# Recommender cross network on one core: first chunk in two halves with the weights loaded between them, clock products on a constant, two products moved into the last wait

## The chip, the cores and the metric

One core of a Trainium2 chip. The metric is the device time of one execution in microseconds (us); lower is better. Every execution is listed with its time and with the span from its first to its last instruction; the time is 1.75 to 1.98 us more than the span. All executions here are of the state "fast".

## The reference, cut to what matters

```python
B, F, D, L = 16384, 26, 16, 6        # Din = 416
x = x0
for l in range(L):
    proj = jnp.einsum('bd,de->be', x, ws[l]) + bs[l]
    x = x0 * proj + x
return x
```

All tensors are bf16. The kernel holds x with the 416 features on partitions, as three tiles of 128 (t = 0, 1, 2) and a tail of 32, and works on 8 groups of 2048 rows, each of four chunks of 512 rows.

## The kernel before

A small scheduler takes instructions with what they read and write and derives the waits; a PSUM bank is one unit of dependence. The front: load the first chunk in two halves, then the first layer's weights; keep TensorE busy with products of ones until data come, so that its clock rises; transpose the first chunk, copy it out of PSUM, and start the products of the first two output tiles.

```python
load_nat(0, 0, 2)                    # chunk 0, rows k = 0, 1 of each four: 208 KB
load_nat(0, 2, KK)                   # chunk 0, k = 2, 3: 208 KB
load_wm(0, "sp")                     # weights of layer 0: 312 KB
for j in range(1, NJ): ...           # chunks 1 to 3, in halves
...
def keep_busy(n, b):                 # clock products, up to four blocks of 128 columns at once
    ... h.matmul(bank(b, ...), ones[:, :], ones[:, :].unsqueeze(1).broadcast_to([P, m, P]), start=True, stop=True),
        reads=["ones"], writes=[("ps", b)]
keep_busy(22, 7)
def first_job():
    transposed_chunk(0)              # 6 transposes, keep_busy(2), 6 transposes, 3 copies of 512 columns
    ...                              # 7 small transposes of the bias, one copy
    keep_busy(5, 3)
    full(g, l, 0, ba, True, True, chunks=[0])      # 3 products of 512 columns
    full(g, l, 1, bb, True, True, chunks=[0])      # 3 more
    transposed_chunk(1)              # 12 transposes, 3 copies
    transposed_chunk(2)
    full(g, l, 0, ba, True, True, chunks=[1]) ...
```

The back, the last layer of the last group, with rows on partitions, so that the result can be stored without a transpose: four rounds kk of four sums; each sum is three products of 416 columns (one per t) and two thin ones. ScalarE copies each sum out (nat_out), VectorE multiplies by x0 and adds x (nat_mul, nat_add), and a store follows each round.

```python
turn_tails(b0); nat_rows(0, bks[0], False)
turn_last(0, b1); turned_out(0, b1)  # 8 transposes that wait for the last additions of the tile before; a copy on VectorE
for j in range(NJ):
    if j == 2: turn_last(2, b2)
    nat_full(0, j, bks[0][j], False, (2,)); nat_out(0, j, bks[0])
turned_out(2, b2)                    # a copy of 1024 columns on ScalarE
...
for kk in range(1, KK):
    nat_rows(kk, bks[kk])
    for j in range(NJ):
        nat_full(kk, j, bks[kk][j], False); nat_out(kk, j, bks[kk]); ...
```

## Time and profile before

| | before |
|---|---|
| median of the first 3 executions | 475.43 us (475.24 to 475.45) |
| median of 6, when the change was measured (those 3 and 3 more) | 475.44 us (475.13 to 476.41) |
| the execution that was profiled | 477.81 us, span 476.0 us |
| TensorE busy | 99% of the span |

### The profile page before, as it was taken

To read this page: it belongs to the slowest core of one execution; us is meant where nothing else is said; L and a number is where in the kernel's file an instruction comes from. 1 tells how busy PE (TensorE), PEld (TensorE's weight loads), DVE (VectorE), ACT (ScalarE), POOL (GpSimd) and SP (SyncE) were. 2 spreads that over 40 slices of the span, in tenths; PEclk is the share of its full clock that TensorE was granted. 3 is DMA by queue.
4 is the path that set the end of the run, shared out by engine and by line. 5 is a ranking of instruction groups with operands and counts; after the bars stand their busy time and mean duration, and the time that the engine had idled before them with its cause. 6 is when DMAs were issued, how large, how long until landed. Compare 5 with 4: busy or idle time off the path is not lost.

```text
span 476.0 us, 8464 instructions
## 1 busy us (share of the span) xinstructions
PE 470.3 (99%) x3407; PEld 200.9 (42%) x3407; DVE 404.2 (85%) x699; ACT 342.0 (72%) x372; POOL 6.3 (1%) x15
## 2 busy tenths in 40 slices
PE   8999999999999999999999999999999999999996
PEld 4434444654444444444444444444444444444442
DVE  1798888888888888898889869988888888888897
ACT  3677777777777777777777777777777777777776
POOL 1000000000000000000000000000000000001000
PEclk9999999999999999999999999999999999999999
DMA  8986830650001398469409940890001029125899
GB/s 223 171 173 143 185 88 1 110 113 1 19 16 30 65 240 147 67 134 239 111 12 170 240 102 10 175 289 2 1 1 35 0 56 232 34 45 101 222 175 288
DMA packets 138651, 53.18 MB, mean 112 GB/s; under 512 B 112362, under 2 KB 138100, under 8 KB 138612
## 3 DMA queue, kind: packets, MB, share of 16 engines
q1 hardware_dynamic: 138456, 52.54, 49.9%
q8 instruction: 26, 0.43, 0.4%
q14 instruction: 13, 0.11, 0.1%
q10 hardware_dynamic: 156, 0.11, 0.1%
HBM read 5.97 MB, written 13.63 MB: 41 GB/s over the span
## 4 chain that ended last, share of the span: by engine, by line
PE 96%; DMA 2%; ACT 1%; DVE 1%; SPq 0%; issue 0%; DVEq 0%
PE ps L471 78%; PE ps L492 7%; PE ps L513 7%; PE ps L868 1%; PE ps L486 1%; DMA wm<-in_ws_dram 1%; ACT tw L398 1%; PE ps L504 1%; PE ps L592 1%; DMA ot<-x 1%; DVE tw L407 0%; PE ps L879 0%; ACT x L923 0%; DVE x L929 0%; DVE x L935 0%; PE ps L912 0%
## 5 line engine op out<-in xcount | busy, mean ns | idle before, releaser
L398 ACT ACTIVATE tw<-ps,bias 128x1024 bf16<-128x1024 f32 (+1 forms) x295 | 299.8, 1071 | 119.5 <-PE ps L492 81.1
L471 PE MATMUL ps<-x,wm 128*128 128x512 bf16 (+1 forms) x1755 | 380.9, 373 | 0.5 <-DMA wm<-in_ws_dram 0.5
L471 PEld LDWEIGHTS ps<-x,wm 128*128 128x128 bf16 x1755 | 165.3, 98 | 210.0 <-issue 29.3
L407 DVE TENSOR_TENSOR tw<-tw,x 128x1024 bf16<-128x1024 bf16 (+1 forms) x285 | 192.7, 684 | 51.8 <-ACT tw L398 51.2
L412 DVE TENSOR_TENSOR x<-tw,x 128x1024 bf16<-128x1024 bf16 (+1 forms) x285 | 182.6, 681 | 0.0
L492 PE MATMUL ps<-x,w 32*128 32x512 bf16 x512 | 39.2, 379 | 0.0
L513 PE MATMUL ps<-x,wm 128*32 128x512 bf16 x564 | 33.0, 380 | 0.0
L438 ACT ACTIVATE ts<-ps,bias 128x512 bf16<-128x512 f32 x47 | 28.8, 701 | 0.0
L442 DVE TENSOR_TENSOR x<-ts,x 128x512 bf16<-128x512 bf16 x47 | 18.7, 419 | 3.9 <-DMA x<-x 3.8
L513 PEld LDWEIGHTS ps<-x,wm 128*32 128x32 bf16 x564 | 13.8, 96 | 17.6 <-issue 5.3
L492 PEld LDWEIGHTS ps<-x,w 32*128 32x128 bf16 x512 | 7.8, 92 | 26.9 <-issue 26.4
L440 DVE TENSOR_TENSOR ts<-ts,x 128x512 bf16<-128x512 bf16 x47 | 18.6, 419 | 0.0
L602 DVE COPY x<-ps 128x512 bf16<-128x512 bf16 x5 | 2.0, 423 | 10.7 <-PE ps L592 10.7
L712 POOL COPY ost<-ot 128x512 bf16<-128x512 bf16 x6 | 4.8, 805 | 424.3 <-DMA ot<-x 424.3
L868 PE MATMUL ps<-wm,x 128*128 128x416 bf16 x48 | 9.5, 340 | 0.0
L604 ACT ACTIVATE x<-ps 128x512 bf16<-128x512 bf16 x7 | 3.8, 595 | 7.4 <-PE ps L592 7.4
L923 ACT ACTIVATE x<-ps 128x416 bf16<-128x416 f32 x16 | 7.8, 526 | 1.6 <-PE ps L868 1.5
L868 PEld LDWEIGHTS ps<-wm,x 128*128 128x128 bf16 x48 | 4.3, 98 | 4.2 <-issue 1.0
L504 PE MATMUL ps<-x,w 32*32 32x512 bf16 x188 | 5.9, 374 | 0.0
L486 PE MATMUL ps<-x,w 32*32 32x512 bf16 x208 | 5.6, 385 | 0.0
L929 DVE TENSOR_TENSOR x<-x,x 128x832 bf16<-128x832 bf16 (+1 forms) x10 | 4.9, 502 | 0.6 <-ACT x L923 0.4
L935 DVE TENSOR_TENSOR x<-x,x 128x832 bf16<-128x832 bf16 (+1 forms) x9 | 4.7, 540 | 0.2
(41 smaller groups left out, 35.4 us busy)
## 6 DMA issues: line engine op xcount, KB each, us to landing
out_dram<-ost SPq DMA_DIRECT2D x6, 1664.0 KB, 7.0
x<-x SPq DMA_DIRECT2D x24, 96.0 KB, 2.1
wm<-in_ws_dram SPq DMA_DIRECT2D x6, 312.0 KB, 3.4
x<-in_x_dram SPq DMA_DIRECT2D x8, 208.0 KB, 4.8
x<-in_x_dram SPq DMA_DIRECT2D x4, 416.0 KB, 8.3
out_dram<-ost SPq DMA_DIRECT2D x2, 832.0 KB, 5.5
x<-x SPq DMA_DIRECT2D x22, 64.0 KB, 2.0
out_dram<-x SPq DMA_DIRECT2D x3, 416.0 KB, 4.1
```

The source lines that it names most:

```text
L398: add("act", lambda h, a=a, w=w, b0=b0: h.activation(tw[r][:, a * CH:(a + w) * CH], psum[:, b0 * CH:(b0 + w) * CH], ACT_F.Identity, bias=b ...
L407: add("dve", lambda h, a=a, e=e: h.tensor_tensor(tw[r][:, a * CH:e * CH], tw[r][:, a * CH:e * CH], x0s[s0][:, i * GC + a * CH:i * GC + e * ...
L412: add("dve", lambda h, a=a, e=e: h.tensor_tensor(xs[so][:, i * GC + a * CH:i * GC + e * CH], tw[r][:, a * CH:e * CH], src(i, a, e), ALU.ad ...
L438: add("act", lambda h: h.activation(ts[r][:, :], bank(b), ACT_F.Identity, bias=bias[:, 3, l:l + 1], scale=1.0), reads=[("ps", b), "bias"], ...
L440: add("dve", lambda h: h.tensor_tensor(ts[r][:, :], ts[r][:, :], x03, ALU.mult), reads=[("ts", r)] + tok0, writes=[("ts", r)], release=True)
L442: add("dve", lambda h: h.tensor_tensor(x3s[so][:, :], ts[r][:, :], res, ALU.add), reads=[("ts", r)] + rtok, writes=[("x3", so), ("x3", so, ...
L471: add("pe", lambda h, t=t, j=j, k=k, w=w: h.matmul(bank(banks[j])[:, k * w:(k + 1) * w], wm[l][:, t, ecols], src(t, j, j + 1)[:, k * w:(k ...
L486: add("pe", lambda h, q=q, j=j, r=r, c=c, o=o: h.matmul(psum[o, banks[j] * CH:(banks[j] + 1) * CH], w3[l][q, i * P + c * T32:i * P + (c + ...
L492: add("pe", lambda h, q=q, j=j, r=r: h.matmul(bank(banks[j]), w3[l][q, ecols], src[q, :], start=first and not inner, stop=not first and no ...
L504: add("pe", lambda h, l=l, b=b, s3=s3, ri=ri, qi=qi, ro=ro, qo=qo: h.matmul(psum[qo, b * CH:(b + 1) * CH], w3[l][qi, NT * P:D], s3[qi, :], ...
L513: add("pe", lambda h, t=t, j=j, src=src, l=l, b=b, ro=ro, qo=qo: h.matmul(psum[qo, b * CH:(b + 1) * CH], wm[l][:, t, NT * P:D], src(t, j, ...
L868: add("pe", lambda h, t=t: h.matmul(bank(b, n=D), xcol(t, j, kk), wm[l][:, t, :], start=(first and t == 0), stop=(not first and t == NT - 1)),
```

## The change

Its intent, as far as the diff shows it: let TensorE start real products before the second half of the first chunk is there, start the clock products without waiting for Pool's ones, and put two products of the second round into TensorE's wait for the last tile.

```diff
     load_nat(0, 0, 2)
+    load_wm(0, "sp")
     load_nat(0, 2, KK)
-    load_wm(0, "sp")
...
     def keep_busy(n, b):
+        one = nc.const_aps.tensor(1.0, [P, CH], BF16)
...
-                bank(b, n=m * P).rearrange("p (m c) -> p m c", m=m), ones[:, :],
-                ones[:, :].unsqueeze(1).broadcast_to([P, m, P]), start=True, stop=True),
-                reads=["ones"], writes=[("ps", b)])
+                bank(b, n=m * P), one[:, 0:P], one[:, 0:m * P], start=True, stop=True), writes=[("ps", b)])
-    keep_busy(22, 7)
+    keep_busy(25, 7)
...
-        transposed_chunk(0)
+        first_half(0)               # 6 transposes, 3 copies of 256 columns
...
-        keep_busy(5, 3)
+        keep_busy(4, 3)
-        full(g, l, 0, ba, True, True, chunks=[0])
-        full(g, l, 1, bb, True, True, chunks=[0])
+        half_products(0, ba[0], 0)  # 3 products of 256 columns
+        first_half(1)
+        half_products(1, bb[0], 0)
+        half_products(0, ba[0], 1)
+        half_products(1, bb[0], 1)
...
     nat_rows(0, bks[0], False)
+    nat_full(1, 1, bks[1][1], True, (0, 1))    # two products of round 1, taken out of it below
     turn_last(0, b1)
```

More of the change, by code (lines that the diff above doesn't have):

```diff
@@ L583, in transposed_chunk @@
     def transposed_chunk(j):
-        ba, bb = ((0, 1), (3, 0), (6, 7), (0, 1))[j]
+        ba, bb = ((3, 0), (6, 7), (0, 1))[j - 1]
         s = slot(0)
-        place = ((ba, 0), (bb, 0), (ba, CH)) if j == 0 else ((ba, 0), (ba, CH), (bb, 0))
+        place = ((ba, 0), (ba, CH), (bb, 0))
         for k2 in (0, 2):
@@ L594, in transposed_chunk @@
                         reads=[("nat", j, k), x0_tok(nat, 0, 0), "ident"], writes=[("ps", b)])
-            if j == 0 and k2 == 0:
-                keep_busy(2, 3)
         for t in range(NT):
@@ L604, in transposed_chunk, with half_cols, first_half, half_products @@
                 add("act", lambda h, dst=dst, sp_=sp_: h.activation(dst, sp_, ACT_F.Copy), **kw)
+    HC = CH // 2
+    def half_cols(t, h):
+        return slice(t * GC + h * HC, t * GC + (h + 1) * HC)
+    def first_half(h):
+        ba, bb = ((0, 1), (5, 6))[h]
+        s = slot(0)
+        place = ((ba, 0), (bb, 0), (ba, HC))
+        for t in range(NT):
+            b, o = place[t]
+            for k in (2 * h, 2 * h + 1):
+                c = slice(o + (k - 2 * h) * P, o + (k - 2 * h + 1) * P)
+                add("pe", lambda h_, t=t, k=k, b=b, c=c: h_.transpose(
+                    psum_t(b)[:, c], x0n[:, 0, k, t * P:(t + 1) * P], ident[:, :]),
+                    reads=[("nat", 0, k), x0_tok(nat, 0, 0), "ident"], writes=[("ps", b)])
+        for t in range(NT):
+            b, o = place[t]
+            dst, sp_ = x0s[s][:, half_cols(t, h)], psum_t(b)[:, o:o + HC]
+            kw = dict(reads=[("ps", b)], writes=[("x0h", t, h)] + ([x0_tok(s, t, 0)] if h else []))
+            if b == bb:
+                add("act", lambda h_, dst=dst, sp_=sp_: h_.activation(dst, sp_, ACT_F.Copy), **kw)
+            else:
+                add("dve", lambda h_, dst=dst, sp_=sp_: h_.tensor_copy(dst, sp_), **kw)
+    def half_products(i, b, h):
+        s = slot(0)
+        for t in range(NT):
+            add("pe", lambda h_, t=t: h_.matmul(
+                bank(b)[:, h * HC:(h + 1) * HC], wm[0][:, t, i * P:(i + 1) * P], x0s[s][:, half_cols(t, h)],
+                start=(t == 0 and h == 0), stop=False),
+                reads=[("x0h", t, h), ("wm", 0)], writes=[("ps", b)])
     def transposed_tails(b):
@@ L907, in turn_tails, with nat_rows @@
             j += n
-    def nat_rows(kk, bks, first=True):
+    def nat_rows(kk, bks, first=True, begun=()):
         for j in range(NJ):
@@ L912, in nat_rows @@
             add("pe", lambda h, j=j, q=q, r=r: h.matmul(
-                bank(bks[j], n=D), x3col(j, kk), w3[l][q, :], start=first, stop=False, tile_position=(r * T32, 0)),
+                bank(bks[j], n=D), x3col(j, kk), w3[l][q, :], start=first and j not in begun, stop=False, tile_position=(r * T32, 0)),
                 reads=tok3 + [("w3", l, r)], writes=[("ps", bks[j])])
@@ L970, in bass_standalone__cross_network_dcn__recsys_kernel @@
     for kk in range(1, KK):
-        nat_rows(kk, bks[kk])
+        begun = (1,) if kk == 1 else ()
+        nat_rows(kk, bks[kk], begun=begun)
         for j in range(NJ):
-            nat_full(kk, j, bks[kk][j], False)
+            nat_full(kk, j, bks[kk][j], False, (2,) if j in begun else range(NT))
             nat_out(kk, j, bks[kk])
```

## The prediction

> **What bounds the kernel now.** I read the page first, for the share of each engine and for the chain that ended last; then the chain and the timeline of the first 17 us and of the last 15 us, because the order of instructions shows the same ones in both kernels between the first chunk of group 0 and the closing stage.
>
> ```profile
> PE 470.3 (99%) x3407; PEld 200.9 (42%) x3407; DVE 404.2 (85%) x699; ACT 342.0 (72%) x372; POOL 6.3 (1%) x15
> PE 96%; DMA 2%; ACT 1%; DVE 1%; SPq 0%; issue 0%; DVEq 0%
> ```
>
> TensorE is the bound from about 6.5 us to about 470 us. The change takes no product out of that stretch: nearly the same products run, some cut in two. So only the two ends, some 6.5 us and 6 us, can move. This is the chain of waits at the front:
>
> ```profile
> 1.65 4.67 DMA wm<-in_ws_dram
> 6.46 2.72 PE ps L471 x6
> 9.18 1.97 PE ps L592 x24
> 11.16 1.29 PE ps L471 x6
> ```
>
> The first products wait for the weights: issued at 1.65 us, 4.67 us under way, landed at 6.32. Then six products of 512 columns take 2.72 us, while the next six of the same kind take 1.29 us. TensorE thus runs at half speed at first. The timeline shows the rest of it:
>
> ```profile
> 0.99 2.53 PE L572 MATMUL ps<-ones 128*128 128x512 bf16 x6 [0.99 <-POOL ones L522]
> 3.38 0.82 PE L592 MATMUL ps<-ident,x 128*128 128x128 bf16 x6
> 4.20 0.85 PE L592 MATMUL ps<-ident,x 128*128 128x128 bf16 x6
> 5.27 0.71 PE L572 MATMUL ps<-ones 128*128 128x512 bf16 x2
> 6.46 2.72 PE L471 MATMUL ps<-x,wm 128*128 128x512 bf16 x6 [0.48 <-DMA wm<-in_ws_dram]
> 8.97 2.18 PE L592 MATMUL ps<-ident,x 128*128 128x128 bf16 x24
> ```
>
> The clock products wait for Pool to write the ones (0.99). Both halves of the first chunk are turned and copied out before the weights come, so only the weights hold PE, with 0.48 us of full idleness. Among the 24 transposes at 8.97 the mean of one changes from 314 to 219 ns at 10.3 us: that is where the clock rises in this execution.
>
> At the back the chain is:
>
> ```profile
> 462.08 0.40 PE ps L879 x4
> 462.48 0.35 PE ps L868 x2
> 462.83 0.65 PE ps L879 x8
> 463.48 0.35 PE ps L868 x2
> 464.30 2.22 PE ps L868 x12
> 470.86 0.53 ACT x L923
> 471.41 0.39 DVE x L929
> 471.81 0.59 DVE x L935
> ```
>
> The transposes of the last tile wait for VectorE's additions (x L412); then three rounds of twelve products run, and at the very end ScalarE and VectorE finish the last quarter.
>
> **What the Trainium skill says.** "TensorE: Matmul & The Clock Gate", Part 1 (the HAM clock gate): the array starts at half rate, a free-running window of about 3.4 us decides, and the point of the rise differs from run to run. The trace agrees on the two rates: 512 columns follow each other at about 0.42 us early (six from 6.46 to 8.97, where the transposes start) and at 0.215 us later (1.29/6). The same page, Part 4 (PE-mode transpose), says that transposes do not count as busy; the trace speaks against that, since the 3.4 us before the rise were 2.0 us of products and 1.4 us of transposes, without a gap. "DMA: Bandwidth & Descriptors", section "Queues, rings and completion order": on each DMA engine descriptors are consumed in ring order. The trace agrees roughly: first half-chunk, second half-chunk, weights landed in the order of issue, at about 3.3, 3.8 and 6.3 us. "PSUM — Partial Sum Buffer", section "The four PSUM rules": the first product of a group clears the marks of its whole bank, which lets the second 256 columns start without the flag; no cost follows from it, and no run so far shows it.
>
> **The change part by part, the front.**
> 1. Weights second in the queue. The issue moves from 1.65 to 1.20 us, and 208 KB fewer lie ahead of it. In the trace the second half-chunk lands some 0.5 us after the first (3.83 against 3.33), so the weights should land about 0.5 us earlier: 6.32 - 0.5 = 5.8 us (estimate). The second half-chunk now follows them. The bytes ahead of the pair's end are unchanged, so it lands where the weights did, about 6.3 us. The loads after them do not move.
> 2. What PE has to do after that. Before: six products at half speed, 2.51 us from 6.46 to 8.97. I take half of one for 256 columns (0.21 us) and a quarter for a transpose of 128 (0.107, as the twelve that start from 8.97 to 10.15 are spaced). After: three products (0.64), six transposes (0.64), and nine more products (1.92): 3.2 us from about 5.97, so 9.17; or, if the second half's landing binds, 6.4 + 0.64 + 1.92 = 8.96. The transposes that were hidden ahead of the weights now lie behind them and eat the gain of 0.5 us: 0 to 0.2 us later.
> 3. Copies. Two VectorE copies of 256 columns and one on ScalarE per half. VectorE took 425 ns for 512 and 683 for 1024, so about 0.30 us for 256; ScalarE 597 and 1030, so 0.38 us (estimates from these rows). Since the dependence is on the whole bank, both VectorE copies wait for the last transpose. At half speed the first products of the second tile (0.64 us) cover this. At full speed they do not (0.33 us), and 0.1 us shows; I make it 0.25 us later then.
> 4. The constant. PE needs no ones from Pool, so it starts at about 0.74 us instead of 0.99; 25 blocks of 128 columns at 0.107 = 2.67 us, ending at 3.40 where before 22 ended at 3.34. Nothing on the path gets shorter by this. Its use is only that the clock may rise earlier. Against that, PE now stands idle from about 4.9 to 5.9 us (half the transposes and one clock product are gone from there), about twice the former gap.
>
> Front without a change in the clock: +0.1 to +0.25 us.
>
> **The back.** Two products of 416 columns (2.22 us for twelve in the chain, so about 0.18 each, 0.35 to 0.37 together) move ahead of the transposes. PE has idle pieces there of about 0.24, 0.09 and 0.11 us, read from the single instructions between 461.6 and 463.1, so they fit nearly whole. They need the last bank that ScalarE empties (about 461.7), hence start some 0.1 us late. The rounds of products then end about 0.32 us earlier. But the ends of the second round are taken by ScalarE, which is held by its copy of 1024 columns until 465.4 and does not move, and VectorE works almost without pause from 466.4. I followed its instructions to the last multiplication that waits for ScalarE, at 471.41: it can come at 471.2. So about 0.15 us of the 0.35 reaches the end.
>
> Sum with an equal clock: +0.15 - 0.15 = 0, in 475.4 us.
>
> **The rivals.** (a) The clock rises earlier. The 9.4 us that PE ran at half rate hold 3.9 us after the weights; full speed there saves at most 1.9 us. For it: if 10.38 us, where the records put the rise, is the end of a window of the skill's 3.41 us, the windows before it are 0.15 to 3.56 and 3.56 to 6.97; in the first PE was busy 2.57 us, 75%, and with the earlier start it is about 83% (0.25 us more of 3.41); if the threshold lies between, the rise comes at 3.56. The next loads allow it: the last half-chunk of the 24 transposes landed at 8.5 us, the next group's data 2 us before use. That gives about 473.5. (b) The clock rises later in more runs, because of the longer gap. The three runs agree within 0.21 us, which may mean that they, unlike the profiled one, rose before 6 us; then losing that costs up to 1.9 us: about 477. (c) The weights do not land earlier, because other transfers slow them: then PE pays the transposes in full, +0.64 us at half speed: 476.0. (d) The moved products in the back save all 0.35 us, if ScalarE's order lets VectorE follow: 475.2.
>
> **Range and chances.** Equal clocks give 475.1 to 475.7, which I hold at about 60%. The earlier start was surely made for the clock, so I give (a) more than (b), and put the point a little below no change, at 475.2 us. The range 473.6 to 476.6 takes in most of (a), all of (c) and half of (b). Two per cent are 9.5 us; both ends together hold not much more than that of waiting, so faster or slower by over 2% are at 0.01 each.
>
> **What would show it.** In the changed profile: clock products from 0.74 us; the weights' wait ended near 5.8 us; an idle piece of about 1 us ahead of the first 256-column products; their last one ended near 9.1 us (right), near 8 us (the clock rose before), or near 9.6 (c). The place at which 314 ns transposes or 634 ns products become 219 and 379 decides (a) and (b). In the back: two products before the transposes and the last ScalarE copy to last VectorE addition shifted by 0.15 us against the last tile's additions. I am wrong if the front gains over 0.3 us at an equal clock, or if the times lie under 474 without an earlier rise.

## The result, and the profile after

The changed kernel took 476.09 us (median of 6, 475.70 to 477.58), the kernel before 475.44 us. The ratio of the fast runs is 1.0014, with a 95% interval from 0.9999 to 1.0030: the same, leaning to slower. Ratios are the mean time of one kernel's fast runs over that of the other's of the same rounds, so not quite the ratio of the medians.

The timeline of TensorE at the front, kernel after (start, length, line, operation, count, and in brackets the length of the wait before it and what ended it; the bias's small transposes and one clock product at 3.86 to 4.5 us are left out):

```profile
0.77 2.82 PE L573 MATMUL ps<-const-bfloat16-1.0 128*128 128x512 bf16 x7 [0.77 <-PEq L1039]
3.39 0.54 PE L617 MATMUL ps<-ident,x 128*128 128x128 bf16 x6
4.45 0.49 PE L632 MATMUL ps<-x,wm 128*128 128x256 bf16 x3
6.11 0.51 PE L617 MATMUL ps<-ident,x 128*128 128x128 bf16 x6 [1.16 <-DMA x<-in_x_dram]
6.45 1.38 PE L632 MATMUL ps<-x,wm 128*128 128x256 bf16 x9
7.66 1.50 PE L591 MATMUL ps<-ident,x 128*128 128x128 bf16 x24
9.23 1.25 PE L471 MATMUL ps<-x,wm 128*128 128x512 bf16 x5
```

The weights come early enough for three products at 4.45, and then TensorE waits 1.16 us for the second half. Everything runs at full speed from 3.46 us on, where the records put the rise of the clock: six transposes take 0.51 us, not 0.82. And yet this execution (476.10 us) is slower than a usual one of before.

One thing must be known before a start is read off such a line. The last one counts five products, but the kernel issues six: a few matmul records are missing from most traces. The same instructions by engine, kernel after, from 8.9 to 10.25 us (PEld is the weight load that goes ahead of each product):

```profile
L471 PEld LDWEIGHTS ps<-x,wm x6: 96/98/99, 8.9 to 9.9; 128*128 128x128 bf16 x6
L471 PE MATMUL ps<-x,wm x5: 379/379/390, 9.2 to 10.1; 128*128 128x512 bf16 x5
```

The missing one is the first. In the five profiles that have all six records (before, a_again, e_filled, e_halves_only, e_const_back) the first product starts 0.054 us after its weight load. Here that load is at 8.950, so the first product started at about 9.00 us, directly behind the transposes, and not at 9.23. Starts corrected in this way are marked "about" below.

The chain of waits of the same stretch (start, length, what; pieces of 0.05 us and less are left out):

```profile
1.66 4.40 DMA x<-in_x_dram
6.11 0.52 PE ps L617 x6
6.65 0.30 DVE x L627
7.00 0.83 PE ps L632 x6
7.83 0.57 PE ps L591 x10
8.42 0.77 DVE x L599 x2
9.23 1.25 PE ps L471 x5
```

Where before only the six products stood behind the last of the first three landings, now six transposes, a copy (0.30) and nine half products do. That copy is a real wait: the third of the nine products starts at 6.67 and the fourth at 7.00, where the others follow at 0.11, so TensorE loses 0.22 us. The wait for copies of 0.77 us in the chain comes of the missing record: the product at 9.23 is the second. In a_again, where no record is missing, the second product follows the first after 0.23 us where later ones follow after 0.22, so that wait costs about 0.02 us at most. The back, in the chain of the same kernel (some pieces between them left out):

```profile
460.61 0.45 PE ps L913 x8
461.27 1.75 ACT x L957 x4
463.01 0.92 ACT x L923
464.78 0.60 DVE x L963
465.41 0.59 DVE x L969
...
471.15 0.29 DVE x L969
```

In the place of TensorE's rounds of twelve products (462.1 to 470.3 before) the chain runs through ScalarE's big copy and VectorE: the two moved products took TensorE off it.

### The profile page after: what moved, and what is told of

Same layout as the page of the kernel before. It is cut to its first block, busy times and chain, and to the rows that moved or that the text cites. A ratio compares the mean times of both kernels' runs of the same rounds, so it can differ in the third digit from the quotient of the medians.

```text
span 474.3 us, 8423 instructions
## 1 busy us (share of the span) xinstructions
PE 462.0 (97%) x3358; PEld 199.8 (42%) x3412; DVE 404.9 (85%) x702; ACT 341.7 (72%) x372; POOL 6.2 (1%) x15
## 4 chain that ended last, share of the span: by engine, by line
PE 92%; ACT 3%; DVE 2%; DMA 1%; issue 1%; SPq 0%; DVEq 0%
PE ps L471 76%; PE ps L492 7%; PE ps L513 6%; ACT tw L398 2%; PE ps L486 1%; DMA x<-in_x_dram 1%; DVE x L963 1%; DVE x L969 1%; PE ps L504 1%; ACT x L957 1%; DMA ot<-x 1%; PE ps L591 0%; ACT x L923 0%; PE ps L632 0%; DVE x L599 0%
## 5 line engine op out<-in xcount | busy, mean ns | idle before, releaser
L471 PE MATMUL ps<-x,wm 128*128 128x512 bf16 (+1 forms) x1695 | 370.6, 371 | 5.6 <-issue 3.7
L627 DVE COPY x<-ps 128x256 bf16<-128x256 bf16 x4 | 1.0, 286 | 5.3 <-PE ps L617 5.3
L601 ACT ACTIVATE x<-ps 128x512 bf16<-128x512 bf16 x5 | 2.7, 595 | 2.6 <-PE ps L591 2.6
```

Of the source, the lines that this page charges most:

```text
L471: add("pe", lambda h, t=t, j=j, k=k, w=w: h.matmul(bank(banks[j])[:, k * w:(k + 1) * w], wm[l][:, t, ecols], src(t, j, j + 1)[:, k * w:(k ...
```

## The experiments

Twelve runs were made, two of them of kernels already measured, all correct. "Short mean" is the mean of the executions under 476.5 us, "late" the number over it; why, the first experiment shows. The line was drawn after the times were seen. Three executions over it were profiled whose clock rose late or fell again (477.81 of before, 477.50 of e_noclock, 478.57 of e_swap), but also one, 476.51 of e_front, whose clock rose early, at 4.93 us; for the others a late rise is inferred from the time. The kernel before ran beside each batch of four.

| run | front | clock products | back | median us | late | short mean us | short mean of before, same batch |
|---|---|---|---|---|---|---|---|
| the change | halves | constant | moved | 476.09 | 1 of 6 | 475.96 | 475.54 |
| b_again | old | ones | old | 475.76 | 0 of 6 | 475.82 | 475.68 |
| e_front | halves | ones | old | 476.01 | 2 of 6 | 475.87 | 475.68 |
| e_back | old | ones | moved | 475.75 | 0 of 6 | 475.73 | 475.68 |
| e_const | old | constant | old | 475.71 | 0 of 6 | 475.78 | 475.68 |
| a_again | halves | constant | moved | 475.97 | 0 of 6 | 475.96 | 475.61 |
| e_filled | halves, filled | constant | moved | 476.00 | 0 of 6 | 475.84 | 475.61 |
| e_halves_only | halves, old loads | ones | old | 477.68 | 5 of 6 | 476.09 (one) | 475.61 |
| e_const_back | old | constant | moved | 475.62 | 0 of 6 | 475.55 | 475.61 |
| e_order | halves, reordered | constant | moved | 475.44 | 0 of 5 | 475.52 | 475.49 |
| e_swap | old, loads swapped | ones | old | 478.00 | 5 of 6 | 476.17 (one) | 475.49 |
| e_noclock | old | none | old | 477.50 | 5 of 5 | none | 475.49 |
| e_const_back2 | old | constant | moved | 475.59 | 0 of 5 | 475.55 | 475.49 |

Short executions of one kernel scatter by 0.1 to 0.5 us (standard deviation), so a mean of five or six is good to 0.1 or 0.2 us. "Give or take" is one standard error throughout. Every run is the same as the kernel before within 2%; the differences below are far smaller than that.

**Theory and rivals.** Theory 1: the profile of before was an execution with a late rise of the clock; at an early rise the front of the change costs 0.6 to 0.9 us (after the first four runs put at about 0.45) and the back saves 0.14. Rivals: the profiling costs the 1.8 us; the difference is luck of the clock; the back's gain is lost to a bank.

**b_again.** No edit.

> The kernel before, unchanged, for a second profile. Theory 1 (the profiled execution of before was one in which the clock rose late, at 10.4 us): most executions show a span near 473.6 us (time near 475.4), and a profile of such a one shows the clock rise before 6.5 us and six products of 1.3 us instead of 2.7 at the front. Rival (the profile itself costs 1.8 us): the span of nearly all executions is near 476.0. Either way the ratio to the kernel before is 1.000 within 0.001.

Spans of its six executions: 473.7 to 474.4. TensorE's timeline in its profile, span 474.1:

```profile
5.93 1.45 PE L471 MATMUL ps<-x,wm 128*128 128x512 bf16 x6 [0.39 <-DMA wm<-in_ws_dram]
7.22 2.02 PE L592 MATMUL ps<-ident,x 128*128 128x128 bf16 x24
9.29 1.24 PE L471 MATMUL ps<-x,wm 128*128 128x512 bf16 x5
```

Six products in 1.45 us where the first profile had 2.72; the rise is recorded at 4.59 us, against 10.38. The chain of this one shows another bound:

```profile
3.98 4.70 DMA x<-in_x_dram
8.73 0.51 PE ps L592 x6
9.29 1.24 PE ps L471 x5
```

In this execution of before, the front waits in the end for the last half of the third chunk (landed at 8.68), not for the weights, and the first product of the second chunk started at about 9.07 us (one record of six is missing here too). Theory 1's first part holds: my picture of the front was that of a rare execution. Of the 46 listed executions of the kernel before, 4 are over 476.5 us, all between 477.6 and 478.

**e_front.** The diff's front and its products, with the ones and the back of before.

> The front of the change alone: halves of 256 columns and the weights between them, clock products still on the ones that Pool writes, nothing moved at the back. Theory 1 (the front is what costs): slower than before by 0.6 to 0.9 us, ratio 1.0013 to 1.0019. Rival (front costs what I predicted at an equal clock, 0.1 to 0.25 us, and the rest is clock luck): ratio 1.0002 to 1.0006 in the executions with an early rise, with single executions 1.5 to 2 us longer.

Short executions 475.87 against 475.68, 0.19 us more. Two of six were over the line, but one of them, 476.51, is the one that was profiled, and its clock rose at 4.93 us: it was long with an early rise: the second half landed only at 6.47 us, and the second chunk's first product started at about 9.42 us, against about 9.07 in b_again. Counted with the early ones it makes the difference 0.32 us, give or take 0.18. The ratio was 1.0006 (0.9990 to 1.0022). That is near the rival's range; theory 1's 0.6 to 0.9 us was too large. The traces of all runs give a better sum (below).

**e_back.** Only the two products moved.

```diff
     nat_rows(0, bks[0], False)
+    nat_full(1, 1, bks[1][1], True, (0, 1))
...
-        nat_rows(kk, bks[kk])
+        begun = (1,) if kk == 1 else ()
+        nat_rows(kk, bks[kk], begun=begun)
...                                  # and below, the product of the third tile alone for that sum
```

> The back of the change alone: two products of 416 columns of the second round ahead of the last transposes. Theory 1 (as predicted: VectorE holds the end): 0.10 to 0.20 us faster, ratio 0.9996 to 0.9998. Rival (the wait for the bank that ScalarE empties last takes the gain): no change or slower by up to 0.2 us. Other rival (all of the 0.35 us arrives): ratio 0.9993.

The times do not resolve it (short mean 475.73 against 475.68). The traces do. I measured from the start of ScalarE's copies of the turned tails (x L904 in b_again), right behind its last evacuation of the last tile. The end of VectorE's last addition stood at +11.95 to +11.96 us in all seven profiles without the move and at +11.82 in all seven with it: 0.14 us, as predicted. But the end of the span moved from +14.38 (mean of seven, 14.31 to 14.46) to +14.33 (14.28 to 14.38): 0.05 us, give or take 0.02. The issue of the store of round 2 stayed at +9.51 in both, and so did its landing at about +12.5 to 12.7; only the later ones are issued earlier, by 0.14, and they land behind it. The last store takes 2.00 us to land in the mean of the seven, against 1.91. My reading is that the later stores queue behind the earlier ones: the DMA engines are full from 466 to 470 us, while those are on their way. No run tested it. Stretches of b_again (busy of each engine, then granted clock, DMA share, GB/s):

```profile
466.00:468.00 2.00, 2.00 (x18) 0.84 (x17) 1.93 (x4) 1.88 (x4) 0.00 (x0) 1.00 1.10 333
468.00:470.00 2.00, 2.00 (x12) 0.92 (x10) 1.89 (x6) 1.49 (x3) 0.00 (x0) 1.00 1.08 321
```

The time from issue to landing of the six stores, shortest, median and longest, in b_again:

```profile
DMA to landing us min/median/max: 1.8/2.7/5.1
```

and in e_back, where the shortest, the last one's, has grown:

```profile
DMA to landing us min/median/max: 2.0/2.7/5.1
```

So the gain was taken twice: once by ScalarE and VectorE (0.35 to 0.14), as predicted, and once by the stores (0.14 to 0.05), as not.

**e_const.** Clock products on the constant, 25 ahead instead of 22.

> The constant alone: clock products on the constant from 0.74 us, 25 blocks ahead instead of 22. Theory 1 (it only makes an early rise more frequent): fast executions equal to those of before within 0.1 us, but fewer long ones (at most one of six over 476.2 us). Rival (it raises the clock earlier in every execution and that is worth time): all executions 0.3 us or more faster. Other rival (no influence on the clock): as many long executions as the kernel before has.

No late execution, the short ones no faster (475.78 against 475.68). One batch alone decides nothing about a thing that happens once in ten. Late executions over all runs, e_swap and e_noclock left out: old front with ones 4 of 52, halves with ones 7 of 12 (e_front, e_halves_only; 5 of 12 if 476.51 and 476.62, just over the line, are not counted), old front with the constant 0 of 17, halves with the constant 1 of 23. For the front in halves the difference is clear, though those two runs differ from the four others in more than the constant, and four of the five come from e_halves_only. For the old front it is not: with no effect at all, 0 of 17 beside 4 of 52 would come about one time in three.

**a_again.** No edit: the changed kernel, beside the next three.

> The changed kernel again, on the chip of the next three. Theory 1 (with an early rise of the clock the front of the change costs about 0.45 us, because the second half of the first chunk now lands last of the first three loads, and all of transposes, copies and half products stand behind it; the back gives 0.14): executions with an early rise 0.2 to 0.6 us above those of before, and about one in three or four with a rise after 8 us, at 477 or more. Rival (clock luck alone): the short executions equal those of before within 0.1 us.

Short executions 475.96 against 475.61: 0.35 us, give or take 0.16, within theory 1's range. That speaks against luck of the clock as the only cause, but one batch does not exclude it; all six executions against all eleven give a ratio of 0.9999 (0.9979 to 1.0020), as two of before's were late. With the first measurement (0.42, give or take 0.21) and e_front (0.32) the mean difference at an early rise is 0.36 us, give or take 0.10. No late ones in six, where I had expected one in three or four: that part was wrong, since the constant was there.

**e_filled.** Twelve blocks of clock products in the 1.2 us wait.

```diff
         half_products(0, ba[0], 0)
+        keep_busy(12, 3)
         first_half(1)
```

> The changed kernel with twelve blocks of clock products in the idle piece of about 1.2 us between the first half products and the second transposes. Theory 1 (that idle piece makes the clock rise late in some executions): no execution over 477 us, the short ones as in the changed kernel within 0.15 us; median up to 0.2 us lower than the changed kernel's. Rival (the idle piece has no influence on the clock): long executions as often as in the changed kernel.

No late ones, but none in a_again either, so it tells nothing of the idle piece. In its profile the clock rose at 6.10 us, so the filling ran at half speed and held the second transposes until 6.45 us, although their data were there at 5.98. Inconclusive.

**e_halves_only.** Halves, ones, old back, and the loads in the old order.

> Halves of 256 columns with the loads in the old order (both halves, then the weights), ones from Pool, back as before. Theory 1 (the serial chain of transposes, copies and half products behind the last landing costs, not the order of the loads): the weights land at 5.4 to 6.3 us as in before, the first products of the second chunk start about 3.5 us after that landing, and the kernel is 0.2 to 0.5 us slower than before. Rival (the order of the loads costs): equal to before within 0.1 us.

The weights landed at 5.96 us and the second chunk's products started 3.35 us later, as expected. The time was not: 477.68, since five of six were late. The one short execution (476.09) is 0.5 us over before. TensorE waited 1.31 us for the weights in the profile, with fewer clock products ahead. So the chain behind the last landing can cost without the new order. A single short execution cannot show that the order costs nothing.

**e_const_back.** Old front, constant, moved products.

> The kernel before with the constant and the two moved products, without the halves and with the old order of loads. Theory 1: 0.10 to 0.20 us faster than before, ratio 0.9996 to 0.9998, no execution over 477 us; faster than the changed kernel by 0.5 to 0.8 us. Rival (constant and back are worth nothing): ratio 1.0000 within 0.0001 in the short executions.

None late; short mean 475.55 against 475.61. The sign fits, the size is below what the times resolve. Under the changed kernel's median beside it, it lies by 0.35 us, where theory 1 had 0.5 to 0.8.

**e_order.** The second chunk's transposes ahead of the second half's products.

```diff
+        transposed_chunk(1)
         half_products(0, ba[0], 1)
         half_products(1, bb[0], 1)
-        transposed_chunk(1)
```

> The changed kernel with the twelve transposes of the second chunk moved ahead of the six products of the second half, so that they fill the wait for the copies. Theory 1 (in the changed kernel PE waits for copies behind the landing of the second half, once for the half and sometimes again for the second chunk): the first products of the second chunk start near 8.8 us instead of 9.0 to 9.2, and the short executions are 0.2 to 0.4 us faster than those of the changed kernel (median 475.6 to 475.8). Rival (the waits for copies hide behind the next loads): the same as the changed kernel within 0.1 us.

The median, 475.44, is below what theory 1 gave (475.6 to 475.8), and the waits for copies are gone from the chain. But its profile had the second half landed at 5.56 us, half a microsecond before that of the changed kernel; from that landing to the second chunk's first product it took about 2.92 us, against about 2.94 and 2.95 in the two profiles of the changed kernel. So filling the wait of 0.22 us gave nothing that shows: the second six of the twelve transposes had to wait in their turn for the second chunk's other half (landed at 6.76). Why this run's landing was early stays open, and so does whether the order is worth anything; the changed kernel did not run beside it.

**e_swap.** The old front with the weights second among the loads.

> The kernel before with nothing but the weights put second among the loads. Theory 1 (whatever is third of the first three loads lands near 6 us, and what is second near 4.3): weights at 4.2 to 4.7 us, second half at 5.9 to 6.5; all transposes of the first chunk and their copies of 512 columns then stand behind that landing, so executions with an early rise are 0.8 to 1.2 us longer than before, and as PE idles for two microseconds about half of them or more rise late (over 477). Rival (the weights need long by themselves, not their place in the queue): weights at 5 us or later, second half within 0.6 us of them.

Weights at 4.36 us, second half at 6.02: place in the queue decides, as theory 1 said. The one short execution is 0.68 us over before (theory 1: 0.8 to 1.2). Five of six were late, up to 479.06. The profile, of the execution of 478.57 us, shows why that one is longer than any of before. Stretches of one clock window each:

```profile
1.21:4.62 3.41, 3.24 (x13) 1.27 (x11) 0.00 (x0) 1.49 (x2) 0.29 (x1) 1.00 0.83 223
4.62:8.03 3.41, 1.93 (x19) 0.96 (x20) 0.42 (x1) 1.17 (x3) 0.44 (x1) 1.00 0.95 327
8.03:11.44 3.41, 3.41 (x26) 2.60 (x25) 0.76 (x2) 0.60 (x1) 0.00 (x0) 0.50 1.11 188
```

The third column is TensorE's busy time, the last but two the granted clock (1.00 also where there is no record, as before the first rise). The clock rose at 4.62; in the window after that TensorE was busy only 1.93 us of 3.41, with 1.61 us waiting for the second half; and the clock fell back to half for the next whole window. So here an early rise was lost again after a wait of 1.61 us, in a window that was 57% busy. In the changed kernel's profile the window after the rise, with its wait of 1.16 us, was 66% busy, and the clock stayed:

```profile
3.46:6.87 3.41, 2.25 (x28) 1.39 (x25) 0.71 (x4) 0.91 (x3) 0.45 (x1) 1.00 1.01 275
```

**e_noclock.** Before without any clock product.

> The kernel before without any clock product. Theory 1 (a window of 3.4 us has to be about 77% busy for the rise, and the transposes alone with the wait for the weights do not fill one): every profile and nearly every execution has the rise after 8 us, and the time is 477.3 to 478.5, 1.8 to 2.8 us over before. Rival (the rise comes in any case by about 6 us): within 0.3 us of before.

All five late, 477.14 to 478.38, two microseconds over before: this is what the clock products are worth. The two windows up to the rise at 10.12 us:

```profile
3.30:6.71 3.41, 2.56 (x22) 1.75 (x23) 0.42 (x1) 1.17 (x3) 0.44 (x1) 1.00 0.93 286
6.71:10.12 3.41, 3.41 (x22) 2.31 (x21) 0.42 (x2) 0.21 (x1) 0.00 (x0) 1.00 1.16 252
```

Busy 75% was not enough, 100% was. The expectation's 77% is not confirmed: in the first profile of before the window from 3.56 to 6.97 was 86% busy (2.93 us) and did not raise the clock. The changes of the clock in e_swap lie 3.41 us apart. Counted back by that from the rise, the window before it began at 1.18 us in b_again and held no wait, while in the first profile of before the windows began at 0.14 and 3.56, and each held one (TensorE stood still until 0.99 us, and for 0.48 us before the products). So the place of the windows may be what makes an execution of the same kernel early or late; no run varied it.

**e_const_back2.** e_const_back once more.

> The constant and the moved products on the old front, a second time on another chip or occasion. Theory 1: short executions 0.1 to 0.2 us faster than the short ones of before, none over 477 us; median at or below 475.65. Rival (the first result was luck of landings): no difference in the short ones, and as many long ones as before.

None late, but 475.55 against 475.49 in the short ones: over both runs no gain is to be seen in the times, only no late executions in 11, and in this batch before had none in 11 either. The rival is half right. This version is the soundest of those tried, with a median 0.35 us under the changed kernel's beside it (475.62 and 475.97); that it beats the kernel before is not shown, nor that it has fewer late executions.

**The sum from the profiles with an early rise (3.5 to 6.7 us).** Start of the second chunk's first product, corrected for missing records: old front about 9.07, 8.56, 8.65, 8.45, 8.97 (b_again, e_back, e_const, e_const_back, e_const_back2), mean 8.74; the change's front about 9.00, 8.99, 9.42 (the change, a_again, e_front), mean 9.14. The front costs about 0.40 us (give or take 0.19), the back returns 0.05; 0.35 is close to the 0.36 of the short executions. That the front is where the profiles differ is well shown: in all fourteen of them, from 473.5 to 476.8 us long, what follows this first product takes 464.8 to 465.3 us.

Three things make the 0.40. The last of the first three loads lands later: 6.06, 6.04, 6.47 against 5.79, 5.60, 5.42, 5.50, 5.94 for the weights before, 0.54 us in the means. From there to the 24 transposes of the next chunks it takes 0.11 longer, which the wait of 0.22 for the copy accounts for: 1.60, 1.61, 1.61 us against 1.50 in the mean of the five (1.43 in b_again; 1.69 in e_const_back2, where the clock rose only at 6.65). And 0.25 is won back, because in the change these transposes run without a pause (1.34 us), while in the old front they take 1.59 in the mean, most in b_again (1.85) and e_const (1.80), which wait for a later load.

How much of the 0.54 belongs to the change is not settled. The order of the three loads is the same in more runs than these eight. Over all fourteen profiles the last of them lands at 6.02 us in the new order (six, 5.56 to 6.47) and at 5.78 in the old (eight, 5.42 to 6.33): 0.24 us, give or take 0.16.

## Why the prediction was right or wrong

- **The class and the range** were right: 476.09 us lies in 473.6 to 476.6, and the ratio is within 2%. The point, 475.2, leaned to the wrong side, and 476.09 is outside the 475.1 to 475.7 that I gave equal clocks. The range held because I had priced both clock rivals, and that is partly luck: the value lies where rival (c) put it, 476.0, but what (c) supposed, weights that land no earlier, did not happen.
- **Front, step 1 (landings).** Wrong for the weights: 4.32 and 4.22 us, not 5.8. Being second they landed two microseconds earlier than in the first profile (6.32), not 0.5. About right for the second half: 6.06 and 6.04, not 6.3. The first error cost nothing, because TensorE waits for the second half anyway.
- **Front, step 2 and 3 (work behind the landing).** The mechanism was right: hidden transposes and copies come out behind the last landing. What it added behind the landing was sized about right, 0.11 us in the means and 0.17 against b_again. The sum was not: +0.1 to +0.25 us predicted, about 0.40 in the profiles. The term that failed is the comparison: I let the second half land "where the weights did, about 6.3 us", from the one profile in which the weights landed late; in the five others of the old front with an early rise they landed at 5.42 to 5.94, so that the last landing moved back by 0.54 us in the means where I had 0. With all profiles it is 0.24, and how much is luck of landings stays open. Step 3's 0.1 us for copies at full speed measured 0.22.
- **Front, step 4 (the constant).** Start at 0.77 us (predicted 0.74), idle 1.16 us (predicted about 1). Rival (a) came true in the profile, the rise at 3.46 us (predicted 3.56) in a window that was 79% busy (predicted 83%), and bought nothing, because the second part of rival (b) held too: usual executions of the old front rise at 4.6 to 5.2 us (b_again, e_back), before the weights come. I had the sign for it in the table, 477.81 us for the profiled execution against 475.43, and used it only as a possibility.
- **Rival (b)**, more late rises, held for the front in halves without the constant (7 of 12, or 5) and not with it (1 of 23).
- **Back.** Predicted 0.15 us at VectorE's end, measured 0.14, with the predicted chain through ScalarE's big copy. The failed step is the last: "0.15 us of the 0.35 reaches the end". The end of the span is the last store's landing, and of the 0.14 only 0.05 us reached it. Rival (d) is out.

## What to carry to other kernels

Look at the time of the profiled execution beside the median before reading its profile: if it is longer, ask which state it shows. Compare the counts of weight loads and products before you take the start of a group from a trace: one missing record moved it by 0.2 us here, more than half of the effect. A load moved forward moves another one back; count what stands behind the one that is now last, and whether it stood in a wait before. At the end of a kernel follow a gain to the last landing of the last store, not to the last instruction that computes.

## What the Trainium skill lacked or had wrong

- "TensorE: Matmul & The Clock Gate", Part 1 and its list of goals: warns of gaps over about 3 us, and of a whole idle window. In e_swap a wait of 1.61 us in a window busy 1.93 of 3.41 us was followed by half the clock for a window; in the changed kernel 2.25 of 3.41 us kept it.
- The same page, Part 4: transposes do not count as busy in the same way. In e_noclock the window before the rise held products for about 1.7 us only (6.71 to 8.39) and then transposes, and the clock rose; in the first profile of before, a window with 2.35 us of products (0.99 to 3.34) did not raise it. So here transposes counted, at least in part.
- The same page gives no share of a window that is needed. Here a window busy 79% raised the clock, two of 75% did not, and one of 86% (3.56 to 6.97 in before) did not either: the profile's busy time, which includes the end of each product and all of the transposes, is not quite what is counted.
- "DMA: Bandwidth & Descriptors" has the order within an engine, but not what it means for three loads in a row: 312 KB of weights landed 3.0 to 3.5 us after their issue when second and 3.8 to 4.7 when third; the other 208 KB 2.5 to 2.8 when second and 3.9 to 4.8 when third.
- No page that I read gives the difference between this device time and the span from the first to the last instruction: 1.75 to 1.98 us in every execution listed with both. Nor does one say that matmul records can be missing: the page of b_again counts 3407 weight loads and 3353 products, that of before 3407 of each.
